# Linear attention plus MLP on one core: two more tiles turned without TensorE, and a normalisation moved to ScalarE

## The chip, the cores and the metric

The kernel runs on one core of one Trainium2 chip. The metric is device time in microseconds of one execution; a kernel's time is the median over several runs. A profiled execution has a time of its own, and inside it a span, from the first to the last recorded instruction.

## The reference

With `x` of 2048 tokens by 512 features, everything in float32:

```python
xn = layernorm(x)                                   # eps 1e-5, no scale, no shift
q, k, v = split(xn @ wqkv)                          # 32 heads of 16
phi = lambda t: where(t > 0, t + 1, exp(t)) + 1e-6
kv, z = sum_s phi(k)_s v_s^T, sum_s phi(k)_s        # per head
o = (phi(q) @ kv) / (phi(q) . z + 1e-6)
h = relu(xn @ w1 + b1) ** 2                         # 512 -> 1376
out = x + o @ wo + h @ w2 + b2
```

## The kernel before, in words

The tokens are 16 tiles of 128. Matrix products are done in three passes: each operand is split into a high half in the matmul's format and the rest (low half), and high x high, high x low and low x high are summed. So most operands have two instructions on the way to TensorE: a copy on ScalarE (`high`, the token tile's copy in `tokens`, the copy in `parts`) and a subtraction on VectorE or GpSimd.

The program first runs through the keys, tile by tile (lines 434 to 646), then through queries, attention and MLP. Only the key stage is touched. For one tile i it needs:

- statistics of the row (`measure`, L214 and L215, VectorE), the reciprocal root by Ln and Exp (`roots`, L225 and L226, ScalarE) with a Newton step on three narrow VectorE instructions (L234 to L236), and the normalisation itself, L242 on VectorE, into `xp[i]`;
- the turned tile (features on partitions): tiles 0 to 7 by four TensorE transposes into PSUM (`turned_pe`, L276), tiles 8 to 15 by `regroup` and `turn`: 16 moves between SBUF places for four tiles at once (`xg<-xp`, issued on SP at L258, 64 KB each), which put 32x32 blocks where they belong, and then one VectorE transpose of 32x32 blocks per tile (L262). `NPE` = 8 is that border;
- the turned tile's high half (`high`, L290, ScalarE) and low half (`low`, L293, VectorE), and for tiles 0 to 7 a copy to DRAM for later (`keep_t`, a ScalarE copy and an SP DMA at L299);
- `project` (L327): 12 matmuls into `pk`, the keys;
- `phi` on them: Relu (L318) and Exp (L320) on ScalarE, a sum on VectorE (L322), into `k`, and its halves in `parts` (L108 and L335);
- the token tile's halves in `tokens` (L108 ScalarE, L116 GpSimd), with the last column replaced by one and zero (L314, a small cast on GpSimd), which yields z;
- `kx` (L346): 12 matmuls that add phi(k)^T times the tokens into four banks. For tiles 0 to 7 they are ordered high x high, high x low, low x high, four each.

Each engine takes its instructions in the order in which the program issues them; a scheduler is switched off (`manual_schedule`). The loop at L610 writes that order out by hand: in round i TensorE projects tile i and does `kx` of tile i - 1; ScalarE does Relu, the high half of the next tile, Exp and the roots, and so on. `ahead` (L606) says of which tiles the statistics are taken at the end of a round, to be normalised in the next. `move(n)` (L255) puts up to n pending moves into SP's queue at the end of a round. `x4` and `x8` hold tiles 4 to 7 and 8 to 11 of the input; the load of `x4` is held back by a small GpSimd copy (L498). Buffers named `t` and `k` share six slots (tag `p`).

Of the kernel before, what the change touches and what calls it, by code (L numbers as in the profile page):

```python
# [18 lines left out]
def kernel(  # L19
# [29 lines left out]
    nc = tc.nc  # L49
    xf = x.rearrange("b s d -> (b s) d")  # L50
    of = out.rearrange("b s d -> (b s) d")
    S, D = xf.shape
    F = w1.shape[1]
    NT = S // P
    NJ = D // P
    TB = 4
    NB = NT // TB
    BT = TB * P
    NF = -(-F // P)
    NPE = 2 * TB  # L60
    WARM = 11
    NP = NF // 2
    FP = NF * P
# [5 lines left out]
    keep = ctx.enter_context(tc.tile_pool(name="keep", bufs=1))  # L69
    work = ctx.enter_context(tc.tile_pool(name="work", bufs=1))  # L70
# [35 lines left out]
    def copy(eng, o, i, bias=0.0):  # L106
        if eng == "act":
            nc.scalar.activation(o, i, AF.Copy, bias=bias)  # L108
        elif bias:
            ENG[eng].tensor_scalar(o, i, bias, None, op0=OP.add)  # L110
        else:
            ENG[eng].tensor_copy(o, i)

    def split(h, l, src, eh, el):
        copy(eh, h, src)
        ENG[el].tensor_tensor(out=l, in0=src, in1=f32(h), op=OP.subtract)  # L116
# [19 lines left out]
    xT = {b: keep.tile([P, NJ, BT], F32, name=f"xT{b}", tag=f"xT{b}") for b in range(NB // 2, NB)}  # L136
# [9 lines left out]
    heads = work.tile([P, P], F32, name="heads", tag="heads")  # L146
    b1s = keep.tile([P, NF], F32, name="b1s")
    zb = keep.tile([P, D], F32, name="zb")
    consts = keep.tile([P, 3, 1], F32R, name="consts")
    one_zero, eps = consts[:, :2], f32(consts[:, 2])  # L150

    xr, xp, xg, tok, pk, kp = {}, {}, {}, {}, {}, {}

# [53 lines left out]
    def group(*tiles):  # L207
        return tiles, *(small.tile([P, 3, k], F32, name=f"{n}{tiles[0]}", tag=n) for n, k in (("st", 6), ("mv", 2), ("y", 3)))
# [19 lines left out]
    def normalise(tiles, st, mv, y):  # L228

        n = len(tiles)  # L230
        var = mv[:, :n, 1]
        y0, u, r = (y[:, k, :n] for k in range(3))

        nc.vector.scalar_tensor_tensor(u, var, 1e-5, y0, op0=OP.add, op1=OP.mult)  # L234
        nc.vector.scalar_tensor_tensor(u, u, -0.5, y0, op0=OP.mult, op1=OP.mult)
        nc.vector.scalar_tensor_tensor(r, u, 1.5, y0, op0=OP.add, op1=OP.mult)  # L236
        for k, i in enumerate(tiles):
            o, src = xp[i], xr[i]
            if i >= NPE:

                o, src = o.rearrange("p g (j c) -> p g j c", j=NJ), gjc(src)
            nc.vector.tensor_scalar(o, src, mv[:, k, 0:1], r[:, k:k + 1], op0=OP.subtract, op1=OP.mult)  # L242
            if i in groups:
                regroup(*groups[i])

    def regroup(src, G):

        for r in range(NJ):
            for g in range(NJ):
                moves.append((G[32 * g:32 * (g + 1), r], src[32 * r:32 * (r + 1), g]))  # L250
        return G
# [8 lines left out]
    def turn(o, G):  # L260

        nc.vector.transpose(o.rearrange("p j (r t) -> p r j t", r=NJ),  # L262
                            G.rearrange("p r (j c) -> p r j c", j=NJ))

    def slot(i):
        return slice((i % TB) * P, (i % TB + 1) * P)

    def cols(i):

        return xsb[(i // TB + 1) % 2]  # L270

    def turned_pe(i):
        p = bank(f"pt{i}", "acc" if i < 3 else "ps")
        for j in range(NJ):
            at_j = slice(j * P, (j + 1) * P)
            nc.tensor.transpose(p[:, at_j], xp[i][:, at_j], ident)  # L276
        return p.rearrange("p (j t) -> p j t", j=NJ)

    def transposed(i, t=None):

        b, at = i // TB, slot(i)
        if i < NPE:
            t = t or turned_pe(i)
        else:
            t = xT[b][:, :, at]
            turn(t, xg[i])
        h, l = (x[:, :, at] for x in cols(i))

        def high():
            nc.scalar.activation(h, t, AF.Copy)  # L290

        def low():
            nc.vector.tensor_tensor(out=l, in0=t, in1=f32(h), op=OP.subtract)  # L293

        def keep_t():
            if i < NPE:
                k = w512(f"t{i}", "p", 6).rearrange("p (j t) -> p j t", j=NJ)
                copy("act", k, t)
                nc.sync.dma_start(xTd[b][:, :, at], k)  # L299

        return high, low, keep_t

    def run(*what):
        for f in what:
            f()

    def tokens(i):
        tok[i] = pair(f"tok{i}")
        h, l = tok[i][:, 0], tok[i][:, 1]
        src = xp[i]  # L310
        if i >= NPE:
            h, l, src = gjc(h), gjc(l), src.rearrange("p g (j c) -> p g j c", j=NJ)
        split(h, l, src, "act", "pool")
        nc.gpsimd.tensor_copy(tok[i][:, :, D - 1:], one_zero)  # L314

    def phi(ps, p, mid=lambda: None, late=lambda: None):

# [130 lines left out]
    nc.gpsimd.memset(f32(one_zero[:, 0]), 1.0)  # L448
    nc.gpsimd.memset(f32(one_zero[:, 1]), 0.0)
# [9 lines left out]
    pw = bank("warm")  # L459
    for _ in range(WARM):  # L460
        nc.tensor.matmul(pw[:, :P], lhsT=zb[:, :P], rhs=zb[:, :P], start=True, stop=True)

    groups = {}
    x4, x8 = four("x4", "r1"), four("x8", "r2")
    for i0 in range(0, NT, TB):
        a = first_xp[i0]
        if i0 < NPE:
            for k in range(TB):
                xp[i0 + k] = a[:, k]
        else:  # L470
            o = four(f"xg{i0}", "r0" if i0 + TB == NT else "r3")
            a, o = (t.rearrange("p a (g c) -> p (a g c)", g=NJ) for t in (a, o))
            groups[i0 + TB - 1] = [t.rearrange("p (g n) -> p g n", g=NJ) for t in (a, o)]
            a, o = (t.rearrange("p (g i c) -> p g i c", g=NJ, i=TB) for t in (a, o))
            for k in range(TB):
                xp[i0 + k], xg[i0 + k] = a[:, :, k], o[:, :, k]

    def heads_k(*js):
        for j in js:
# [63 lines left out]
    load_x(12, two("x12"))  # L543
    load_x(14, two("x14"))
    project(2, pks[2], wk, HL)
    soon = group(4, 8, 9)
    phi_k(0, pks[0])
    measure(soon, 0)
    tokens(0)
    parts(0)  # L550
    keep2()
# [51 lines left out]
                held.pop(0)()  # L603
            fetch()

    ahead = {3: (5, 10), 4: (6, 11), 5: (7, 12), 6: (13, 14), 7: (15,)}  # L606

    kxp = [bank(f"kx{c}", "acc") for c in range(NJ)]
    kx(0)
    for i in range(2, NT):  # L610
        if i == NPE:
            wq = both("wq", ("B0", "B1"))
        if i == 3:
            nc.sync.dma_start(b1s[:, :NF - 1], b1[:(NF - 1) * P].rearrange("(f p) -> p f", p=P))
# [6 lines left out]
        if i + 1 < NPE:  # L621
            high, low, keep_t = transposed(i + 1)
        k = NPE if i + 1 == NPE else i + 2
        turned = transposed(k) if i + 1 >= NPE and k < NT else ()

        def late():
            if soon:
                roots(*soon)
            low()

        phi_k(i, ps, high, late)
        run(*turned)
        if soon:
            normalise(*soon)
        parts(i)
        keep_t()
        if i == 2:
            tokens(2)
        if i + 1 < NT:
            tokens(i + 1)  # L640
        if i + 1 == NPE:
            run(*transposed(NPE + 1))
        pieces(2 if i >= NPE else 0)
        soon = statistics(*ahead[i + 1]) if i + 1 in ahead else ()
        move(8 if i >= NPE - 1 else 16)
        kx(i - 1)
# [98 lines left out]
    last = TB - 1  # L745
    w2r = [four(f"w2r{k}", f"C{k}", F32R, keep) for k in range(2)]
    for n in range(2):
        t1, t2 = NB - 1 - 2 * n, NB - 2 - 2 * n
        x1, x2 = xsb
        tag = "acc" if n else "ps"  # L750
# [207 lines left out]
        f = NF - 2  # L958
# [34 lines left out]
        for e, f in enumerate(waiting[:-2]):  # L993
# [22 lines left out]
            if e == NF - 4:  # L1016
                turned = attention_T(t2 * TB + 2)
# [53 lines left out]
```

## Time and profile before

| | |
|---|---|
| time, median of 3 runs | 424.54 us (423.74 to 424.91) |
| the profiled execution's own time | 423.9 us |
| its span | 422.2 us |
| TensorE matmul busy | 417.2 us, 99% of the span |
| VectorE, ScalarE, GpSimd busy | 71%, 59%, 8% |
| granted TensorE clock | 1.0 |
| DMA | 43.02 MB, 16 engines busy 34.4% on the main queue |

In the rows of a time line the columns are start, duration, engine, line, operation, result <- sources, the shapes and the count; in brackets stands the idle time of that engine just before, and what ended it. PE is TensorE's matmuls, PEld its weight loads, DVE VectorE, ACT ScalarE, POOL GpSimd, SPq the queue that issues DMAs. Several instructions of a kind in a row are merged into one row with their count. In a row of stretches, the first number is the length, then each engine's busy time and count of instructions, the granted clock, the busy share of the DMA engines and GB/s. The chain of work gives start, duration and what it was. In a row of groups the last part is busy time, mean ns of one, and idle time before with its releasers. A row of DMA issues ends with the microseconds from issue to landing.

### The profile page before, as it was taken

The page shows a single profiled execution, that of the slowest core. Times are in us where ns is not written, and L with a number is a line of the kernel's source. Part 1 is how long each engine was busy: PE and PEld are TensorE (multiplying, and loading weights), DVE is VectorE, ACT ScalarE, POOL GpSimd, SP SyncE. Part 2 cuts the span into 40 slices and gives each one's busy share as a digit, 9 for nine tenths or more (in the row PEclk, how much of TensorE's full clock was granted, in tenths as well). Part 3 has the DMA queues.
Part 4 walks back from the last instruction along what each step waited for, and adds up shares of the span by engine and source line. Part 5 has one row for each costly group of instructions (what it writes and reads, how often), then busy time and mean ns, then how long its engine had stood idle before and what let it go on. Part 6 is the DMA issues. An engine that isn't in the chain of part 4 may idle for free.

```text
span 422.2 us, 5377 instructions
## 1 busy us (share of the span) xinstructions
PE 417.2 (99%) x1868; PEld 344.8 (82%) x1868; DVE 299.0 (71%) x537; ACT 248.9 (59%) x441; POOL 33.2 (8%) x52
## 2 busy tenths in 40 slices
PE   8999999999999999999999999999999999999996
PEld 7788888888887888888888888888888888888885
DVE  6897788855668886777579376586977668577353
ACT  5766667645467777566466363666667665556140
POOL 3342333330000000000000000000000000000000
PEclk9999999999999999999999999999999999999999
DMA  7853437000412221536016652501120654023502
GB/s 248 282 157 82 105 105 230 16 0 2 112 50 63 88 73 52 184 84 182 0 57 196 190 201 76 144 0 50 51 75 25 200 99 152 1 88 96 160 0 99
DMA packets 42754, 43.02 MB, mean 102 GB/s; under 512 B 5828, under 2 KB 28612, under 8 KB 42472
## 3 DMA queue, kind: packets, MB, share of 16 engines
q1 hardware_dynamic: 42728, 42.69, 34.4%
q8 instruction: 14, 0.23, 0.2%
q14 instruction: 12, 0.10, 0.1%
HBM read 30.09 MB, written 6.29 MB: 86 GB/s over the span
## 4 chain that ended last, share of the span: by engine, by line
PE 97%; DVE 1%; DMA 1%; POOL 0%; ACT 0%; issue 0%; POOLq 0%
PE acc L127 38%; PE b L419 23%; PE kx L346 10%; PE pq L327 10%; PE pk L327 10%; PE pz L127 1%; PE b L127 1%; PE pkv L730 1%; PE pt L276 1%; PE pm L127 1%; DMA x<-in_A_x_dram 1%; PE end L127 0%; DVE st L214 0%; POOL tok L116 0%; DVE xp L242 0%; ACT k L320 0%
## 5 line engine op out<-in xcount | busy, mean ns | idle before, releaser
L127 PE MATMUL acc<-w2r,s 128*128 128x512 f32 x498 | 116.6, 389 | 0.0
L127 PEld LDWEIGHTS acc<-w2r,s 128*128 128x128 f32 x498 | 93.5, 188 | 19.6
L419 PE MATMUL b<-T,aop 128*128 128x512 f32 x240 | 59.6, 389 | 0.0
L419 PEld LDWEIGHTS b<-T,aop 128*128 128x128 f32 x240 | 45.0, 188 | 9.4
L346 PE MATMUL kx<-pk,tok 128*128 128x512 f32 x192 | 47.3, 394 | 0.1
L346 PEld LDWEIGHTS kx<-pk,tok 128*128 128x128 f32 x192 | 35.4, 188 | 8.3 <-POOL tok L314 1.1
L127 PE MATMUL acc<-mh,aTsr 128*128 128x512 f32 x96 | 30.3, 390 | 0.0
L108 ACT ACTIVATE w2r<-r 128x512 fp32r<-128x512 f32 x32 | 20.0, 625 | 13.5 <-PE acc L127 10.4
L119 DVE TENSOR_TENSOR w2r<-r,w2r 128x512 fp32r<-128x512 f32 x32 | 21.9, 686 | 7.3 <-ACT w2r L108 7.2
L419 PE MATMUL b<-xs0h,aop 128*128 128x512 f32 x80 | 26.4, 391 | 0.0
L116 POOL TENSOR_TENSOR tok<-xp,tok 128x512 fp32r<-128x512 f32 x16 | 22.1, 1379 | 53.6 <-ACT tok L108 53.6
L116 DVE TENSOR_TENSOR s<-c,s 128x512 fp32r<-128x512 f32 x20 | 13.9, 693 | 16.7 <-ACT s L108 16.7
L199 POOL MEMSET r<- 32x512 f32 x3 | 1.6, 522 | 278.1 <-DVE w2r L119 278.0
L322 DVE SCALAR_TENSOR_TENSOR q<-pq,q 128x512 f32<-128x512 f32 x16 | 11.0, 689 | 16.8 <-ACT q L320 16.8
L108 ACT ACTIVATE aop<-S 128x512 fp32r<-128x512 f32 x20 | 12.6, 629 | 14.7 <-DVE S L659 9.4
L127 PEld LDWEIGHTS acc<-mh,aTsr 128*128 128x128 f32 x96 | 18.0, 188 | 3.8
L860 DVE TENSOR_TENSOR res<-acc,res 128x512 f32<-128x512 f32 x16 | 11.0, 692 | 13.7 <-PE acc L127 13.7
L318 ACT ACTIVATE q<-pq 128x512 f32<-128x512 f32 x16 | 9.5, 591 | 18.4 <-PE pq L327 18.4
L318 ACT ACTIVATE k<-pk 128x512 f32<-128x512 f32 x16 | 9.5, 594 | 16.6 <-PE pk L327 16.5
L127 PE MATMUL acc<-ml,aTsr 128*128 128x512 f32 x48 | 18.7, 390 | 0.0
L419 PEld LDWEIGHTS b<-xs0h,aop 128*128 128x128 f32 x80 | 15.0, 188 | 3.4 <-ACT rz L407 0.3
L262 DVE STREAM_TRANSPOSE at<-g 128x512 f32<-128x512 f32 x16 | 10.5, 690 | 7.3 <-DMA g<-q 7.3
(190 smaller groups left out, 840.3 us busy)
## 6 DMA issues: line engine op xcount, KB each, us to landing
r<-in_B_w_dram SPq DMA_DIRECT2D x49, 256.0 KB, 3.2
res<-in_A_x_dram SPq DMA_DIRECT2D x8, 512.0 KB, 6.1
g<-q SPq DMA_DIRECT2D x64, 64.0 KB, 2.1
out_dram<-res SPq DMA_DIRECT2D x15, 256.0 KB, 2.1
x<-in_A_x_dram SPq DMA_DIRECT2D x5, 512.0 KB, 5.5
xTd<-t SPq DMA_DIRECT2D x8, 256.0 KB, 3.3
rq<-in_A_wqkv_dram SPq DMA_DIRECT2D x8, 256.0 KB, 5.9
xg<-xp SPq DMA_DIRECT2D x32, 64.0 KB, 2.0
```

The source lines that it names most:

```text
L108: nc.scalar.activation(o, i, AF.Copy, bias=bias)
L116: ENG[el].tensor_tensor(out=l, in0=src, in1=f32(h), op=OP.subtract)
L119: nc.vector.tensor_tensor(out=l, in0=src, in1=f32(h), op=OP.subtract)
L127: nc.tensor.matmul(ps, lhsT=a[u], rhs=b[v], start=first and n == 0, stop=last and n == 2)
L262: nc.vector.transpose(o.rearrange("p j (r t) -> p r j t", r=NJ), G.rearrange("p r (j c) -> p r j c", j=NJ))
L276: nc.tensor.transpose(p[:, at_j], xp[i][:, at_j], ident)
L318: nc.scalar.activation(p, ps, AF.Relu, scale=-1.0)
L322: nc.vector.scalar_tensor_tensor(p, ps, 0.0, p, op0=OP.max, op1=OP.add)
L327: nc.tensor.matmul(ps, lhsT=cols(i)[u][:, j, slot(i)], rhs=w[v][:, j, :], start=first and n == 0, stop=last and n == len(steps) - 1)
L346: nc.tensor.matmul(kxp[c], lhsT=tok[i][:, u, c * P:(c + 1) * P], rhs=pk[i][:, v], start=i == 0 and (u, v) == first, stop=i == NT - 1 and ( ...
L419: nc.tensor.matmul(ps, lhsT=a[u][:, j * P:(j + 1) * P], rhs=b[v][:, j, :], start=first and j == 0 and n == 0, stop=last and j == 1 and n == 2,
L860: nc.vector.tensor_tensor(out=r[:, a:z], in0=ps, in1=r[:, a:z], op=OP.add)
```

## The change

- Tiles 6 and 7 (`NDVE` = 6 up to `NPE` = 8) are normalised into a grouped layout, moved by 16 moves of 32 KB, and turned by VectorE into a buffer of tag `p`, which also goes to DRAM, so that the ScalarE copy for that is left out. Their eight TensorE transposes go.
- Tiles 8 to 15 are normalised on ScalarE: Identity with a scale and a bias per partition, the bias being -mean x reciprocal root, from one more narrow VectorE instruction per group. They are put at the end of the round's ScalarE work.
- The statistics come in other rounds: first 4, 6, 7 (was 4, 8, 9), then `ahead` as in the diff.
- Tile 8 is turned in round 6 (was round 7), 9 and the following in the round two before their own.
- The last column of a token tile is set to one by a GpSimd memset of `xp` before the halves are made, instead of a cast after them; the low half is then zero by itself. For tiles turned by TensorE it follows the transposes; for the others it comes with the tile before and waits for the moves that read it.

```diff
+    NDVE = NPE - 2
...
+        if tiles[-1] >= NPE:
+            nc.vector.scalar_tensor_tensor(u, mv[:, :n, 0], -1.0, r, op0=OP.mult, op1=OP.mult)
+        later = []
+
+        def last(i, o, src, k):
+            nc.scalar.activation(o, src, AF.Identity, bias=u[:, k:k + 1], scale=r[:, k:k + 1])
+            if i in groups:
+                regroup(*groups[i])
+
         for k, i in enumerate(tiles):
             o, src = xp[i], xr[i]
-            if i >= NPE:
+            if i >= NDVE:
                 o, src = o.rearrange("p g (j c) -> p g j c", j=NJ), gjc(src)
-            nc.vector.tensor_scalar(o, src, mv[:, k, 0:1], r[:, k:k + 1], op0=OP.subtract, op1=OP.mult)
-            if i in groups:
-                regroup(*groups[i])
+            if i < NPE:
+                nc.vector.tensor_scalar(o, src, mv[:, k, 0:1], r[:, k:k + 1], op0=OP.subtract, op1=OP.mult)
+                if i in groups:
+                    regroup(*groups[i])
+            else:
+                later.append(lambda a=(i, o, src, k): last(*a))
+        return later
...
         if i < NDVE:
             t = turned_pe(i)
         else:
-            t = xT[b][:, :, at]
+            t = xT[b][:, :, at] if i >= NPE else w512(f"t{i}", "p", 6).rearrange("p (j t) -> p j t", j=NJ)
             turn(t, xg[i])
...
+    def ones(i):
+        nc.gpsimd.memset(xp[i][:, D - 1:] if i < NDVE else xp[i][:, NJ - 1, P - 1:], 1.0)
...
         split(h, l, src, "act", "pool")
-        nc.gpsimd.tensor_copy(tok[i][:, :, D - 1:], one_zero)
+        if NDVE <= i + 1 < NT:
+            ones(i + 1)
...
-    soon = group(4, 8, 9)
+    soon = group(4, 6, 7)
...
-    ahead = {3: (5, 10), 4: (6, 11), 5: (7, 12), 6: (13, 14), 7: (15,)}
+    ahead = {3: (5, 8, 9), 4: (10, 11), 5: (12, 13), 6: (14, 15)}
...
-        k = NPE if i + 1 == NPE else i + 2
-        turned = transposed(k) if i + 1 >= NPE and k < NT else ()
+        turned = transposed(i + 2) if NDVE <= i + 1 and i + 2 < NT and i + 2 != NPE else ()
...
         run(*turned)
-        if soon:
-            normalise(*soon)
+        later = normalise(*soon) if soon else []
         parts(i)
         keep_t()
+        if i + 2 == NPE:
+            run(*transposed(NPE))
...
         if i + 1 < NT:
             tokens(i + 1)
-        if i + 1 == NPE:
-            run(*transposed(NPE + 1))
+        if i + 2 == NDVE:
+            run(*transposed(NDVE))
+        run(*later)
```

More of the change, by code (lines that the diff above doesn't have):

```diff
@@ L148 @@
     zb = keep.tile([P, D], F32, name="zb")
-    consts = keep.tile([P, 3, 1], F32R, name="consts")
-    one_zero, eps = consts[:, :2], f32(consts[:, 2])
+    eps = keep.tile([P, 1], F32, name="eps")
     xr, xp, xg, tok, pk, kp = {}, {}, {}, {}, {}, {}
@@ L276, in turned_pe, with transposed @@
             nc.tensor.transpose(p[:, at_j], xp[i][:, at_j], ident)
+        ones(i)
         return p.rearrange("p (j t) -> p j t", j=NJ)
-    def transposed(i, t=None):
+    def transposed(i):
         b, at = i // TB, slot(i)
-        if i < NPE:
-            t = t or turned_pe(i)
+        if i < NDVE:
+            t = turned_pe(i)
         else:
-            t = xT[b][:, :, at]
+            t = xT[b][:, :, at] if i >= NPE else w512(f"t{i}", "p", 6).rearrange("p (j t) -> p j t", j=NJ)
             turn(t, xg[i])
@@ L296, in keep_t @@
             if i < NPE:
-                k = w512(f"t{i}", "p", 6).rearrange("p (j t) -> p j t", j=NJ)
-                copy("act", k, t)
+                k = t
+                if i < NDVE:
+                    k = w512(f"t{i}", "p", 6).rearrange("p (j t) -> p j t", j=NJ)
+                    copy("act", k, t)
                 nc.sync.dma_start(xTd[b][:, :, at], k)
@@ L310, in tokens @@
         src = xp[i]
-        if i >= NPE:
+        if i >= NDVE:
             h, l, src = gjc(h), gjc(l), src.rearrange("p g (j c) -> p g j c", j=NJ)
         split(h, l, src, "act", "pool")
-        nc.gpsimd.tensor_copy(tok[i][:, :, D - 1:], one_zero)
+        if NDVE <= i + 1 < NT:
+            ones(i + 1)
     def phi(ps, p, mid=lambda: None, late=lambda: None):
@@ L447 @@
                             pattern=[[-1, P]], channel_multiplier=1)
-    nc.gpsimd.memset(f32(one_zero[:, 0]), 1.0)
-    nc.gpsimd.memset(f32(one_zero[:, 1]), 0.0)
     nc.gpsimd.memset(heads, 1.0)
@@ L466 @@
         a = first_xp[i0]
[L467 to L476, printed above, removed]
+        for k in range(TB):
+            xp[i0 + k] = a[:, k]
+        if i0 + TB <= NDVE:
+            continue
+        n = TB if i0 >= NPE else NPE - NDVE
+        o = work.tile([P, n, 512], F32, name=f"xg{i0}", tag="r0" if i0 + TB == NT else "r3" if i0 >= NPE else "ra")
+        a, o = (t.rearrange("p a (g c) -> p (a g c)", g=NJ) for t in (a[:, TB - n:], o))
+        groups[i0 + TB - 1] = [t.rearrange("p (g n) -> p g n", g=NJ) for t in (a, o)]
+        a, o = (t.rearrange("p (g i c) -> p g i c", g=NJ, i=n) for t in (a, o))
+        for k in range(n):
+            xp[i0 + TB - n + k], xg[i0 + TB - n + k] = a[:, :, k], o[:, :, k]
     def heads_k(*js):
@@ L620 @@
         high = low = keep_t = lambda: None
-        if i + 1 < NPE:
+        if i + 1 < NDVE:
             high, low, keep_t = transposed(i + 1)
-        k = NPE if i + 1 == NPE else i + 2
-        turned = transposed(k) if i + 1 >= NPE and k < NT else ()
+        turned = transposed(i + 2) if NDVE <= i + 1 and i + 2 < NT and i + 2 != NPE else ()
         def late():
```

## Prediction

> **What bounds the kernel now.** I read the page first, then the busy time by stretches, then the chain of work that ended last.
>
> ```profile
> span 422.2 us, 5377 instructions
> PE 417.2 (99%) x1868; PEld 344.8 (82%) x1868; DVE 299.0 (71%) x537; ACT 248.9 (59%) x441; POOL 33.2 (8%) x52
> ...
> 20.00:419.00 399.00, 398.95 (x1787) 329.89 (x1785) 283.51 (x499) 235.83 (x415) 27.18 (x35) 1.00 0.32 93
> ```
>
> From 20 to 419 us TensorE is busy 398.95 of 399.00 us at a granted clock of 1.00. So each microsecond taken off TensorE's own list there shortens the span by one, each new wait of TensorE lengthens it by one, and there is no later idle time that could absorb either. The place of the change is the key stage, where the chain alternates between twelve matmuls `pk` of one tile and twelve `kx` of the tile before, with four transposes `pt` between them as long as TensorE turns tiles:
>
> ```profile
> 35.40 2.72 PE pk L327 x12
> 38.12 0.44 PE pt L276 x4
> 38.56 2.75 PE kx L346 x12
> 41.31 2.72 PE pk L327 x12
> ...
> 47.25 2.72 PE pk L327 x12
> ...
> 52.69 2.72 PE pk L327 x12
> 55.41 2.72 PE kx L346 x12
> ```
>
> These `pk` are those of tiles 5, 6, 7 and 8, and the last `kx` is tile 7's. A period with transposes takes 5.91 us (35.40 to 41.31) and 5.94 (41.31 to 47.25), one without 5.44 (47.25 to 52.69).
>
> **Part 1, the transposes of tiles 6 and 7 go.** Both periods become 5.44: 0.47 + 0.50 = **0.97 us** less. Nothing hides this, since TensorE is the bound.
>
> **Part 2, ones by a memset.** Now a GpSimd cast behind the low half of each token tile holds up the first two `kx`:
>
> ```profile
> 15.98 0.63 ACT L108 ACTIVATE pk<-k 128x512 fp32r<-128x512 f32 x1 [0.24 <-DVE k L322]
> 16.67 0.53 PEld L346 LDWEIGHTS kx<-pk,tok 128*128 128x128 f32 x3 [0.18 <-ACT pk L108]
> 16.68 0.98 DVE L335 SCALAR_TENSOR_TENSOR pk<-k,pk 128x512 fp32r<-128x512 f32 x1
> 17.77 0.19 PEld L346 LDWEIGHTS kx<-pk,tok 128*128 128x128 f32 x1 [0.56 <-POOL tok L314]
> 19.43 0.63 ACT L108 ACTIVATE pk<-k 128x512 fp32r<-128x512 f32 x1 [0.23 <-DVE k L322]
> 20.27 0.53 PEld L346 LDWEIGHTS kx<-pk,tok 128*128 128x128 f32 x3
> 21.21 0.19 PEld L346 LDWEIGHTS kx<-pk,tok 128*128 128x128 f32 x1 [0.41 <-POOL tok L314]
> 23.16 0.19 PEld L327 LDWEIGHTS pk<-wkh,xs1h 128*128 128x128 f32 x1
> ```
>
> At 2.72 / 12 = 0.227 a matmul the fourth weight load would come at 17.35 and 20.95; it comes at 17.77 and 21.21, so 0.42 + 0.26 = 0.68 is lost. What is late next: tile 0's fifth matmul needs VectorE's low half, done at 17.66, and tile 1's `kx` needs ScalarE's high half, done at 20.06. So tile 1 starts near 20.13 whatever tile 0 gained, and twelve unhindered matmuls end at 22.85 instead of 23.16: **0.3 us** less, with bounds 0 and 0.68.
>
> The memset for tile 0 now stands on GpSimd ahead of the copy that releases the load of tiles 4 to 7, and waits for tile 0's transposes:
>
> ```profile
> 6.63 0.47 POOL L498 COPY x<-y 128x1 f32<-128x1 f32 x1 [4.03 <-DVE y L236]
> 7.03 0.60 ACT L290 ACTIVATE xs1h<-pt 128x512 fp32r<-128x512 f32 x1
> 15.87 0.68 DVE L214 BATCH_NORM_STATS2 st<-x 128x6 f32<-128x512 f32 x1
> ...
> x<-in_A_x_dram SPq DMA_DIRECT2D x1, 1024.0 KB, 6.6
> ```
>
> So that load leaves about 0.5 us later. With 6.6 us to landing it is there near 14.3, before the statistics at 15.87: nothing. Without that cover it would cost 0.5.
>
> **Part 3, what takes the transposes' place.** Tiles 6 and 7 are normalised where 8 and 9 were, then 16 moves of 32 KB go through SP's queue (ahead of the two bias loads and the stores of turned tiles 4 and 5, all wanted later), and VectorE turns the result. Moves and turns now:
>
> ```profile
> 23.61 1.46 DVE L242 TENSOR_SCALAR xp<-x,mv,y 128x512 f32<-128x512 f32 x3
> 34.55 0.15 DVE L234 SCALAR_TENSOR_TENSOR y<-mv,y 128x2 f32<-128x2 f32 x1
> ...
> 36.05 0.69 DVE L335 SCALAR_TENSOR_TENSOR pk<-k,pk 128x512 fp32r<-128x512 f32 x1
> 36.42 10.10 SPq L258 DMA_DIRECT2D xg<-xp  x16
> ...
> 61.15 4.95 SPq L258 DMA_DIRECT2D xg<-xp  x8
> 67.73 0.71 DVE L262 STREAM_TRANSPOSE xT<-xg 128x512 f32<-128x512 f32 x1 [0.26 <-issue]
> ...
> 180.48 11.77 SPq L258 DMA_DIRECT2D g<-q  x16
> ```
>
> SP issues one move per 0.63 us (10.10 / 16; 4.95 / 8 = 0.62). The last of the eight is issued at 61.15 + 7 x 0.62 = 65.5 and the turn that needs it starts at 67.73: 2.2 us from last issue to turn. Moves of 32 KB are not in this trace: I take 0.63 for them too (the nearest row, same engine, same 32 partitions), with bounds 0.57 (below that the end of VectorE's earlier work decides, see the rivals) and 0.73 (11.77 / 16). Tile 7's normalisation ends at 25.07, less the 0.3 of part 2; the first move goes at about 25.0, so the turn of tile 6 starts at 25.0 + 15 x 0.63 + 2.2 = **36.65**. Tile 6's own projection is wanted at 41.31 - 0.77 = 40.5 and has its high half by 38.1 (prices below): covered.
>
> What is queued behind that turn is the matter. ScalarE's list has, in order: high half of tile 6 (waits for the turn), then its new work, normalising tiles 10 and 11. Only then can the 16 moves of tiles 8 to 11 start, which now start at 36.42. Later, the high half of tile 8 waits for those moves, and behind it ScalarE has the token half of tile 7, the normalising of 14 and 15, and only then tile 7's own Relu and Exp, which TensorE's `kx` of tile 7 needs. Now ScalarE does these two first (50.01, 50.63), ahead of tile 8's half:
>
> ```profile
> 50.01 0.60 ACT L318 ACTIVATE k<-pk 128x512 f32<-128x512 f32 x1 [1.79 <-PE pk L327]
> 50.63 0.63 ACT L320 ACTIVATE k<-k 128x512 f32<-128x512 f32 x1
> 51.30 0.69 DVE L322 SCALAR_TENSOR_TENSOR k<-pk,k 128x512 f32<-128x512 f32 x1 [0.99 <-ACT k L320]
> 51.59 0.62 ACT L290 ACTIVATE xs1h<-xT 128x512 fp32r<-128x512 f32 x1
> 52.11 0.62 ACT L108 ACTIVATE pk<-k 128x512 fp32r<-128x512 f32 x1
> ...
> 55.43 0.70 DVE L262 STREAM_TRANSPOSE xT<-xg 128x512 f32<-128x512 f32 x1
> 56.16 0.63 ACT L290 ACTIVATE xs1h<-xT 128x512 fp32r<-128x512 f32 x1 [2.91 <-DVE xT L262]
> 290.31 0.72 ACT L407 ACTIVATE c<-c,b1s 128x512 f32<-128x512 f32 x1 [1.01 <-DVE c L884]
> 290.94 0.58 ACT L108 ACTIVATE t<-b 128x512 f32<-128x512 f32 x1
> ...
> L407 ACT ACTIVATE c<-c,b1s 128x512 f32<-128x512 f32 x10 | 7.3, 726 | 8.9 <-DVE c L884 8.9
> L108 ACT ACTIVATE tok<-xp 128x512 fp32r<-128x512 f32 x16 | 9.8, 618 | 0.0
> ```
>
> Prices: a turn's reader starts 0.73 after the turn (55.43 to 56.16); independent activations start 0.52 apart (51.59 to 52.11). A normalising activation, with bias and scale both per partition, is not in the trace. One with such a bias takes 0.726 against 0.618 without, 0.63 to the next start; with two I take 0.82 and 0.72 (bounds 0.62 and 0.90). The Trainium skill, "ScalarE: Activation LUTs", What ACT_TABLE_LOAD costs, gives 93 ns for each per-partition operand; the 108 ns above agree roughly, and its estimate of 0.80 would shorten the sum by under 0.1 us.
>
> The sum, from the turn of tile 6 at 36.65: high half +0.73, tile 10 +0.52, tile 11 +0.72, its end +0.82 (39.44); first move +0.1, last move +9.45, turn of tile 8 +2.2 = **51.2**. From there: its high half 51.93 to 52.55, `pk` of tile 8 by 52.68. TensorE wants it at 52.69 - 1.27 = 51.42: 1.26 lost. On ScalarE: tokens 52.45, tile 14 52.97, tile 15 53.69, tile 7's Relu 54.41, Exp 55.03 to 55.66, VectorE's sum 55.70 to 56.39, high half 56.44 to 57.06, `kx` of tile 7 at 57.2 (0.14 as from 15.98 + 0.63 to the first matmul after 16.67). Wanted at 55.41 - 1.27 = 54.14: **3.06 lost** in all, the first 1.26 included. In general the loss is the start of tile 8's turn less 48.14.
>
> Elsewhere: VectorE gives up eight normalisations and gets two turns and a narrow scale column per group. After tile 6's high half (38.0) its list to tile 5's low half has seven wide instructions of up to 0.69 (36.05) and six narrow ones of some 0.15 (34.55): 43.7, where the fifth matmul of tile 5's `kx` is wanted near 44.1, so no wait, with 0.4 to spare. The memsets for tiles 6 and 8 wait on GpSimd until the moves that read those columns have landed (36.5 and 51.1); the token halves behind them come at about 42 and 57. The moves of 12 to 15 now go without a break from 53.69 + 0.82 = 54.5 to 64.6, so a weight load that SP now issues just ahead of 61.15 goes some 4 us later, about when ScalarE, itself late, comes to it: nothing in the sum.
>
> Net: -0.97 - 0.30 + 3.06 = +1.8. The profiled execution took 423.9 around its span of 422.2; it becomes 425.7. The runs' median is 424.54, 0.64 above it, so I forecast **426.3** for the median: +0.42%. A difference of 0.3% (1.27 us) is about what a measurement here can tell from none.
>
> The Trainium skill, "VectorE: DVE Perf Modes", Rules for kernel authors, speaks against the change: it gives a 128x128 transpose to TensorE where PSUM may hold the result. By it the change loses, as in the sum; 0.44 us of `pt` stands against 16 issues of 0.63.
>
> **Rivals.** A, *the other side*: the queue is quick enough. If tile 8's turn can start by 48.1, ScalarE is never held, and the full 1.27 comes off: 423.27. That point needs a pitch of 0.49 per move for tiles 8 to 11 even with the earliest turn of tile 6 (48.1 - 35.7 - 2.9 - 2.2 = 7.3 over 15). For it: ScalarE is busy only 59% of the span. Against: 24 moves in a row at 0.62 to 0.63.
>
> B, smaller moves issue faster: at 0.57 or less the turn of tile 6 waits no longer for them but for VectorE's low half (it starts at 36.05 now, behind two normalisations of together 1.0 that go, and would end near 35.7). Tile 8's turn is then at 35.7 + 2.9 + 9.45 + 2.2 = 50.25, the loss 2.1, the time 425.4. Against: nothing shows that size matters for the pitch.
>
> C, moves at 0.73: tile 6's turn at 38.15, tile 8's at 52.7, the loss 4.56, the time 427.8.
>
> D, the change doesn't do what it says, the transposes being hidden already: the periods of 5.91 and 5.44 speak against it, and I give it nothing.
>
> **How the numbers follow.** Forecast 0.56, A 0.16, B 0.12, C 0.09, and 0.07 for what lies between A and B. Slower by over 0.3%: 0.54 of the forecast and C, 0.63. Faster: A with its startup gain between 0.3 and 0.68, 0.15. Within: B, the middle and the edges, 0.22. The range goes from A's 423.3 to C's 427.9, as the pitch of one move, times fifteen and twice in a row, carries it all.
>
> **What would show it.** Right: no `pt` of tiles 6 and 7; the first weight load of tile 3 near 22.85; 16 small moves over 10 us from 25; tile 8's turn near 51 after a wait for moves; ScalarE idle before that tile's high half, and TensorE waiting on ScalarE at `pk` of tile 8 and `kx` of tile 7, some 3 us together. Wrong: TensorE without idle between 40 and 60 us (A), a shorter pitch of the small moves (B), or waits in another place.

## The result and the profile after

| | before | after |
|---|---|---|
| time, median | 424.31 us (423.74 to 424.91, 4 runs) | 427.47 us (426.94 to 427.86, 4 runs) |
| the profiled execution's own time, its span | 423.9, 422.2 us | 427.3, 425.6 us |

The ratio of the runs is 1.0078, 95% interval 1.0066 to 1.0089; the medians lie 3.2 us apart (1.0074). So it is slower. The forecast was 426.3, 1.8 above the median then known (424.54). The page of the changed kernel begins with the span and the busy time:

```profile
span 425.6 us, 5376 instructions
PE 417.1 (98%) x1860; PEld 344.2 (81%) x1860; DVE 296.9 (70%) x532; ACT 253.0 (59%) x445; POOL 27.5 (6%) x50
```

TensorE's work did not grow; it even lost eight transposes. So the time went into waits. Two stretches of the changed kernel say where (columns: length, then busy time and count of TensorE, weight loads, VectorE, ScalarE and GpSimd, the granted clock, DMA):

```profile
20.00:62.00 42.00, 38.85 (x174) 30.92 (x173) 32.11 (x73) 30.50 (x60) 11.10 (x16) 1.00 0.46 120
62.00:419.00 357.00, 357.00 (x1589) 295.52 (x1588) 247.90 (x418) 209.72 (x360) 11.22 (x18) 1.00 0.31 90
```

All of it lies between 20 and 62 us: 3.15 us without a matmul, and none after 62. The same stretch of the kernel before has no such time:

```profile
20.00:62.00 42.00, 42.00 (x195) 34.46 (x194) 35.43 (x79) 27.57 (x59) 14.67 (x18) 1.00 0.41 110
```

TensorE's time line of the changed kernel in that stretch names the waits. Its rows of `pk` are the first matmuls of tiles 6, 7, 8 and 9:

```profile
40.67 0.39 PE L348 MATMUL pk<-wkh,xs0h 128*128 128x512 f32 x1
...
45.10 2.11 PE L367 MATMUL kx<-pk,tok 128*128 128x512 f32 x8 [0.64 <-DVE pk L356]
47.05 0.40 PE L348 MATMUL pk<-wkh,xs0h 128*128 128x512 f32 x1
...
53.72 0.50 PE L348 MATMUL pk<-wkh,xs1h 128*128 128x512 f32 x1 [1.06 <-ACT xs1h L304]
...
58.19 3.06 PE L367 MATMUL kx<-pk,tok 128*128 128x512 f32 x12 [1.45 <-ACT pk L109]
61.08 0.39 PE L348 MATMUL pk<-wkh,xs1h 128*128 128x512 f32 x1
```

The same work in the kernel before, `pk` of tile 8, `kx` of tile 7 and `pk` of tile 9:

```profile
52.53 0.39 PE L327 MATMUL pk<-wkh,xs1h 128*128 128x512 f32 x1
...
55.25 2.88 PE L346 MATMUL kx<-pk,tok 128*128 128x512 f32 x12
57.97 0.39 PE L327 MATMUL pk<-wkh,xs1h 128*128 128x512 f32 x1
```

A period without transposes takes 5.44 there (52.53 to 57.97), and half of one 2.72. Set beside that, the waits cost 0.94 (tile 5's `kx`, after its first four matmuls: 47.05 less 40.67 is 6.38), 1.23 (tile 8's `pk`), 1.75 (tile 7's `kx`) and 0.17 in its course, together 4.09. Less the 0.97 of the transposes, tile 9's `pk` starts 3.11 later (61.08 against 57.97). The idle times in brackets add up to 3.15 only: each matmul's row lasts 0.39, while the next one starts 0.23 after it, so beside a wait some of the loss counts as busy (4.09 less 3.15 here). That is why the busy time of the page fell by 0.1 only, though 0.97 of transposes are gone. The last matmul ends 3.06 later (422.02 against 418.96) and the span 3.4.

The chain of work that ended last runs through exactly what was put in the transposes' place (start, duration, what):

```profile
34.92 1.88 DMA xg<-xp
...
36.98 0.72 DVE t L275
37.72 0.63 ACT xs0h L304
38.35 1.42 ACT xp L242 x2
...
46.76 1.49 SPq L271
...
50.20 1.97 DMA xg<-xp
...
52.29 0.72 DVE xT L275
...
54.19 1.41 ACT xp L242 x2
```

Read downwards: the last of the small moves lands, tile 6 is turned and its high half made, only then does ScalarE normalise tiles 10 and 11, only then do the moves of tiles 8 to 11 begin, and the last one lands just before tile 8's turn at 52.29. Then comes another pair of normalisations on ScalarE (tiles 14 and 15), ahead of tile 7's Relu. The rows of SP's queue give the pitch:

```profile
25.36 10.14 SPq L271 DMA_DIRECT2D xg<-xp  x16
...
39.79 10.99 SPq L271 DMA_DIRECT2D xg<-xp  x16
```

The first sixteen carry 32 KB each, the second 64 KB: 0.63 us apiece for both, apart from one of the second group that took 1.49. The page lists a DMA queue `q8 instruction`, with 14 packets over the span. One of these is under way when that issue begins (the packet starts at 46.61 and takes 1.27, the issue starts at 46.76).

The first of the three waits is of another kind. The time line of all engines around it:

```profile
43.13 1.30 POOL L117 TENSOR_TENSOR tok<-xp,tok 128x512 fp32r<-128x512 f32 x1 [5.16 <-DVE y L236]
...
43.17 1.27 DVE L238 SCALAR_TENSOR_TENSOR y<-mv,y 128x2 f32<-128x2 f32 x1
...
44.37 0.68 DVE L356 SCALAR_TENSOR_TENSOR pk<-k,pk 128x512 fp32r<-128x512 f32 x1
44.48 1.52 ACT L242 ACTIVATE xp<-x,y 128x512 f32<-128x512 f32 x2 [1.43 <-DVE y L238]
```

A VectorE instruction on 128x2 numbers, 0.16 us elsewhere, takes 1.27 and ends at 44.44, within 0.01 of GpSimd's subtraction (43.13 + 1.30). Tile 5's low half is queued behind it, and ScalarE's normalising waits for it. The Trainium skill, "SBUF — State Buffer", SBUF: two separate sides, says that a VectorE instruction with two inputs in SBUF and a GpSimd one that reads SBUF exclude each other, and that whichever starts first keeps the port to its end. By that rule this trace agrees: 1.27 against 0.16.

### The profile page after: what moved, and what is told of

Same layout as the page of the kernel before. It is cut to its first block, busy times and chain, and to the rows that moved or that the text cites. A ratio compares the mean times of both kernels' runs of the same rounds, so it can differ in the third digit from the quotient of the medians.

```text
span 425.6 us, 5376 instructions
## 1 busy us (share of the span) xinstructions
PE 417.1 (98%) x1860; PEld 344.2 (81%) x1860; DVE 296.9 (70%) x532; ACT 253.0 (59%) x445; POOL 27.5 (6%) x50
## 4 chain that ended last, share of the span: by engine, by line
PE 88%; SPq 4%; DVE 3%; ACT 2%; DMA 1%; issue 1%; DVEq 0%
PE acc L128 38%; PE b L440 22%; PE pq L348 10%; PE pk L348 6%; PE kx L367 6%; SPq L271 4%; PE pz L128 1%; PE b L128 1%; PE warm L480 1%; DMA xg<-xp 1%; PE pkv L752 1%; ACT xp L242 1%; PE pm L128 1%; DVE pk L356 1%; DVE k L343 0%
## 5 line engine op out<-in xcount | busy, mean ns | idle before, releaser
L343 DVE SCALAR_TENSOR_TENSOR k<-pk,k 128x512 f32<-128x512 f32 x16 | 11.0, 685 | 8.9 <-ACT k L341 8.9
```

Source lines behind the costliest of these rows:

```text
L343: nc.vector.scalar_tensor_tensor(p, ps, 0.0, p, op0=OP.max, op1=OP.add)
```

## The experiments

Theory: the loss is the lateness of tile 8's turn. That is 16 issues of 0.63 us on one queue, begun behind ScalarE's normalising, and then ScalarE's in-order list, where tile 8's half and two normalisations stand ahead of tile 7's Relu. Rivals: that the waits add up one by one, that normalising on ScalarE costs by itself, or that the transposes' time was never there to gain. Each ratio below is against runs of the kernel before on the same chip. Lines of kernels with one more constant are shifted by one.

**1. Tile 7's Relu first** (tile 8 turned in round 7, as before):

```diff
-        turned = transposed(i + 2) if NDVE <= i + 1 and i + 2 < NT and i + 2 != NPE else ()
+        k = NPE if i + 1 == NPE else i + 2
+        turned = transposed(k) if NDVE <= i + 1 and k < NT and i + 2 != NPE else ()
...
-        if i + 2 == NPE:
-            run(*transposed(NPE))
...
+        if i + 1 == NPE:
+            run(*transposed(NPE + 1))
```

> From the changed kernel, only the order: tile 8 is turned in round 7 again, so that ScalarE has tile 7's Relu and Exp ahead of tile 8's high half. My theory (the loss is set by the start of tile 8's turn, 52.29 us in the changed kernel's profile, and by what stands behind its high half on ScalarE): the wait of pk of tile 8 stays (1.2 us), that of kx of tile 7 (1.75 us) goes, so about 425.7 us against 427.5. Rival (ScalarE's added load as such costs the time, 8 activations of 0.8): the work is the same, so no change, 427.5.

Measured: 425.56 us, ratio 1.0038 (1.0023 to 1.0053), where the changed kernel has 1.0078. ScalarE's time line of this run:

```profile
50.11 0.57 ACT L339 ACTIVATE k<-pk 128x512 f32<-128x512 f32 x1
50.71 0.63 ACT L341 ACTIVATE k<-k 128x512 f32<-128x512 f32 x1
53.15 0.63 ACT L304 ACTIVATE xs1h<-xT 128x512 fp32r<-128x512 f32 x1 [1.80 <-DVE xT L275]
```

Tile 8's turn still starts at 52.40. But Relu and Exp now stand ahead of the half that waits for it, and tile 7's `kx` waits for nothing. So the 1.75 at that `kx` came from ScalarE's order alone.

**2. Tile 5's parts first** (removes the wait of tile 5's `kx`):

```diff
+        if i == NDVE - 1:
+            parts(i)
         later = normalise(*soon) if soon else []
-        parts(i)
+        if i != NDVE - 1:
+            parts(i)
```

> From the changed kernel, only the order: in round 5 the halves of tile 5's keys stand ahead of the narrow scale instructions on VectorE. The wait of TensorE at kx of tile 5 (1.07 us in the profile) should go in any case. My theory: the time stays at 427.5 within 0.3, since tile 8's turn starts no sooner (52.3) and pk of tile 8 then waits about 2.2 instead of 1.2 us. Rival (each wait of TensorE counts by itself): 426.5.

Measured: 427.35 us, ratio 1.0077 (1.0062 to 1.0092). TensorE's waits in this run (total, times, longest):

```profile
PE pk L348 <- ACT xs1h L304: 1.6, 1, 1.6
PE kx L367 <- ACT pk L109: 1.5, 1, 1.5
```

Tile 5's wait is gone and the time is unchanged. Counted by starts as above, tile 8's `pk` now loses 2.24 instead of 1.23 (it starts 7.68 after tile 7's, 46.39 to 54.07), and tile 7's `kx` 1.75 as before: the waits are not additive. What sets the end is the later of the two, tile 8's turn.

**3. The queue cleared** (ScalarE normalises 10 and 11 ahead of tile 6's half; the store of tile 6 and the bias loads go behind the moves of 8 to 11):

```diff
-        if i + 2 == NDVE:
-            run(*transposed(NDVE))
         run(*later)
+        store_6 = lambda: None
+        if i + 2 == NDVE:
+            h6, l6, store_6 = transposed(NDVE)
+            run(h6, l6)
...
         move(8 if i >= NPE - 1 else 16)
+        store_6()
...
-        if i == 3:
+        if i == NPE:
             nc.sync.dma_start(b1s
```

> From the changed kernel, only the order: on ScalarE the normalising of tiles 10 and 11 stands ahead of tile 6's high half, and on SP the store of turned tile 6 and the two bias loads stand behind the moves of tiles 8 to 11. My theory: these moves start at about 38.0 instead of 39.8 us, tile 8's turn at 50.5 instead of 52.3, so 1.8 us less, 425.7. Rival (ScalarE's added load): the same work, no change, 427.5.

Measured: 425.96 us, ratio 1.004 (1.0026 to 1.0054). Here the moves start at 38.23 and the turn at 51.01:

```profile
38.23 10.08 SPq L271 DMA_DIRECT2D xg<-xp  x16
```

That is 1.28 sooner than in the changed kernel, and this execution began 0.24 later than that of before. The prediction's formula (start of tile 8's turn less 48.14) reckons with a start that is 0.30 sooner, by part 2; this one is 0.24 later. Without the one and with the other it gives 51.01 - 48.14 - 0.30 - 0.24 = 2.33. Tile 7's `kx` starts at 56.90 instead of 55.25, and 56.90 - 55.25 - 0.24 + 0.97 = 2.38. By tile 9's `pk` (59.76 instead of 57.97) the loss is 2.52. The waits are at other places than in the changed kernel: 1.17 at tile 5's `kx`, none at tile 8's `pk`, and 0.77 at tile 7's `kx`.

**4. All normalising back on VectorE**, tiles 6 and 7 still moved:

```diff
+    NACT = 16
...
-        if tiles[-1] >= NPE:
+        if tiles[-1] >= NACT:
...
-            if i < NPE:
+            if i < NACT:
```

> From the changed kernel, tiles 8 to 15 are normalised on VectorE again; tiles 6 and 7 are still turned by moves. My theory: the moves of tiles 8 to 11 still queue on SP behind the store of turned tile 6 (about 38.9), tile 8's turn starts near 50.8, and behind its high half ScalarE has only the tokens: kx of tile 7 at about 55.4 instead of 58.2, so some 2.8 us less, 424.7, not better than before. Rival (ScalarE's load was the whole loss): the transposes' gain shows, 423.3.

Measured: 424.92 us, ratio 1.0021 (1.0011 to 1.003). The moves of 8 to 11 start at 38.56. The wait that TensorE shows is tile 5's `kx`, here because of a normalisation itself. GpSimd's and VectorE's time lines:

```profile
42.78 1.29 POOL L118 TENSOR_TENSOR tok<-xp,tok 128x512 fp32r<-128x512 f32 x1 [4.97 <-ACT tok L110]
...
42.83 2.00 DVE L253 TENSOR_SCALAR xp<-x,mv,y 128x512 f32<-128x512 f32 x2
44.75 0.68 DVE L357 SCALAR_TENSOR_TENSOR pk<-k,pk 128x512 fp32r<-128x512 f32 x1
...
51.05 0.71 DVE L276 STREAM_TRANSPOSE xT<-xg 128x512 f32<-128x512 f32 x1 [1.21 <-DMA xg<-xp]
```

Two normalisations that together take 1.00 at 48.24 take 2.00 here, and tile 5's low half, next in line, makes TensorE wait 1.39. It is not the only thing that is late: tile 8's turn still waits for the moves. In the changed kernel tile 8's `pk` starts 1.43 after that turn (52.29 to 53.72), which would give about 52.5 here (an estimate); it starts at 52.90, behind the late `kx`. So most of this loss would have come at tile 8's `pk` if it had not come before. No wait of TensorE for ScalarE is left, and the time is close to the 424.7 of the theory.

**5. Two queues**: the changed kernel, every second move of 8 to 11 issued by GpSimd.

```diff
-                nc.sync.dma_start(*moves.pop(0))
+                (nc.gpsimd if two and len(moves) % 2 else nc.sync).dma_start(*moves.pop(0))
...
-        move(8 if i >= NPE - 1 else 16)
+        move(8 if i >= NPE - 1 else 16, i == 4)
```

> As the changed kernel, but every second one of the 16 moves of tiles 8 to 11 is issued by GpSimd's queue instead of SyncE's. Theory (16 moves at one every 0.63 us on one queue set the turn of tile 8): the last move goes out about 5 us sooner, tile 8's turn no longer waits (at or under 48), the waits of tile 8's pk and of tile 7's kx are gone and only the wait in tile 5's kx (0.94 us) stays: 424.2 us. No issue on GpSimd's queue shows in any trace so far: if one took over 1.1 us there, the turn would come at 50 and the time would be 425.9 or more. Rival (normalising on ScalarE itself holds TensorE up, whatever the queue): 426.5 to 427.5.

Measured: 425.41 us, ratio 1.0031 (1.002 to 1.0042); 424.2 was expected. The queue's part came true, the rest did not. SP's, GpSimd's and VectorE's time lines:

```profile
39.70 5.32 SPq L271 DMA_DIRECT2D xg<-xp  x8
...
39.98 4.07 POOL L271 DMA_DIRECT2D xg<-xp  x8 [2.06 <-ACT xp L242]
...
43.20 2.71 DVE L356 SCALAR_TENSOR_TENSOR pk<-k,pk 128x512 fp32r<-128x512 f32 x1
...
49.64 0.71 DVE L275 STREAM_TRANSPOSE xT<-xg 128x512 f32<-128x512 f32 x1
```

The last move goes out near 45 instead of 50, the turn waits for no move (no bracket), and the waits of tile 8's `pk` and tile 7's `kx` are gone. But GpSimd's subtraction now comes right behind its issues (44.07 to 45.36) and meets tile 5's low half itself: that begins while GpSimd still issues and ends 0.55 after the subtraction, 2.71 instead of 0.69. By the starts on record this is not the order of the Trainium skill's rule above: the low half began 0.87 before the subtraction. Nor do the issues alone explain it: in run 12 a low half at 41.32, amid GpSimd's issues, took 0.69. What held it at first stays open. Tile 7's `pk` starts 1.86 late and stays so. The Trainium skill, "DMA: Bandwidth & Descriptors", Rules for kernel authors, says that spreading transfers over issuing engines gains no bandwidth and only saves issue time. Here issue time was what was short: 5.32 for SP's eight against 10.99 for sixteen.

**6. The ones alone** (4's edit and the one below, with the rounds and `ahead` of before, so that only the memset is left of the change):

```diff
-    NDVE = NPE - 2
+    NDVE = NPE
+    NACT = NT
```

> The kernel before with the memset of the ones alone; all else as before. Theory: the stretch from the first matmul of tile 0's pk to that of tile 3's is 15.4 us instead of 15.7, as in all five traces with the memset, and that comes out at the end: 0.3 under the kernel before, about 423.7. Rival (the gain of the start is an accident of when tile 0's data arrived, or is given back later): the stretch stays at 15.7, or the time stays at 424.0.

Measured: 423.84 us, ratio 0.9995 (0.9987 to 1.0004): not distinguishable from no change. In the trace the stretch from tile 0's first `pk` matmul to tile 3's is 15.46, against 15.70 (7.68 to 23.38) before:

```profile
8.17 1.02 PE L349 MATMUL pk<-wkh,xs1h 128*128 128x512 f32 x2
...
23.63 0.39 PE L349 MATMUL pk<-wkh,xs1h 128*128 128x512 f32 x1
```

All thirteen traces with the memset have 15.37 to 15.46, so 0.24 to 0.33 are gained there. But where the stretch begins varies from 7.64 to 8.28 among executions of the same start, and that covers it.

**7. VectorE for 8 to 11, and the queue cleared** (the edits of 2 and 3, and 4's with another border):

```diff
+    NACT = 12
```

> Tiles 6 and 7 turned by moves, tiles 8 to 11 normalised on VectorE and 12 to 15 on ScalarE; the store of tile 6 and the bias loads behind the moves of 8 to 11 on SyncE's queue; in round 5 tile 5's pk low half ahead of the normalising. Theory: the moves of 8 to 11 start at 36.2, right behind those of 6 and 7, tile 8's turn comes at 48.3 (0.2 to 0.5 after it would be free of waits), tile 5's kx waits for nothing: 0.97 and 0.3 gained, 0.3 to 0.5 lost to the turn and 0.3 at the last store: 423.4 to 423.7. Rival (the removed transposes were hidden anyway, or VectorE is now too full in rounds 4 and 5): 424.0 to 425.

**8. The same with two queues** (5's edit on top):

```diff
-        move(8 if i >= NPE - 1 else 16)
+        move(8 if i >= NPE - 1 else 16, i == 4)
```

> As the run with tiles 8 to 11 on VectorE and the cleared queue, and every second move of tiles 8 to 11 issued by GpSimd's queue too. Theory: tile 8's turn comes at about 43.5, well ahead of its time; no wait on TensorE from tile 3 on; 0.97 and 0.3 gained, 0.3 lost at the last store at most: 423.0 to 423.2. Rival (the issue on GpSimd's queue delays its subtractions, so that tile 6's kx waits): 424 or more, with a wait of TensorE for GpSimd.

Measured: 424.92 (1.0021, 1.0012 to 1.003) and 425.36 (1.003, 1.0018 to 1.0041); both theories missed. The times fall where the rivals had them, but TensorE waits for ScalarE, which neither rival named, and by the same mechanism in both. In 8 the last move begins to be issued at 41.57, and yet tile 8's turn comes at 49.94. ScalarE's time line in 8:

```profile
45.00 1.52 ACT L243 ACTIVATE xp<-x,y 128x512 f32<-128x512 f32 x2 [2.06 <-DVE y L239]
46.43 0.58 ACT L340 ACTIVATE k<-pk 128x512 f32<-128x512 f32 x1
...
51.75 1.51 ACT L243 ACTIVATE xp<-x,y 128x512 f32<-128x512 f32 x2
53.16 0.57 ACT L340 ACTIVATE k<-pk 128x512 f32<-128x512 f32 x1
```

Tiles 12 and 13 are normalised at 45.00, after a wait for VectorE's narrow instructions (the first of them takes 1.25, beside GpSimd's subtraction again). Tile 6's Relu stands behind them, VectorE's sum and low half of tile 6 behind that (to 49.84), and then the turn. One round on it is the same for tile 7's Relu (53.16), and TensorE waits for ScalarE 0.23 at tile 6's `kx` and 0.99 at tile 7's. So the rival has its share: with the queue out of the way, normalising on ScalarE costs by its place ahead of Relu.

**9. ScalarE's normalising alone** (as 6, with tiles 8 to 15 on ScalarE):

```diff
-    NACT = NT
+    NACT = NPE
```

> The kernel before, with the memset of the ones and with tiles 8 to 15 normalised on ScalarE; tiles 6 and 7 stay with TensorE's transposes and the rounds of the statistics stay as before. Theory (normalising on ScalarE costs TensorE time only where it stands ahead of a Relu that TensorE's next product needs and ScalarE has no idle time left): in the kernel before ScalarE idles 1.8 us ahead of each Relu of rounds 4 and 5, the two normalisations take 1.4, so no new wait shows: 423.7 to 424.0. Rival (it always costs, as the last run suggests): a wait of TensorE for ScalarE's pk of 0.5 to 1.0 in one or two rounds, 424.5 to 425.5.

Measured: 424.47 us, ratio 1.001 (1.0001 to 1.0019), between the two expectations and 0.6 above run 6. No wait in rounds 3 to 9. The one wait is 0.43 at tile 10's `kx`, and it comes through the moves again: those of 12 to 15 start at 57.27 (before: 54.98), and VectorE waits for them at tile 12's turn:

```profile
70.03 0.71 DVE L276 STREAM_TRANSPOSE xT<-xg 128x512 f32<-128x512 f32 x1 [2.28 <-DMA xg<-xp]
```

**10 and 11. All on VectorE, tiles 12 to 15 one round later** (with 3's and 4's edits), on one queue and, with 5's edit, on two:

```diff
-    ahead = {3: (5, 8, 9), 4: (10, 11), 5: (12, 13), 6: (14, 15)}
+    ahead = {3: (5, 8, 9), 4: (10, 11), 6: (12, 13), 7: (14, 15)}
...
+        if i >= NDVE - 1:
+            parts(i)
         later = normalise(*soon) if soon else []
-        parts(i)
+        if i < NDVE - 1:
+            parts(i)
```

> All tiles normalised on VectorE, tiles 6 and 7 turned by moves, SyncE's queue cleared, a round's pk low half ahead of its normalising from round 5 on, and tiles 12 to 15 measured and normalised one round later, so that round 5 has none. Theory (the remaining losses of the last runs are engine time in rounds 5 and 6: ScalarE's 1.4 us ahead of Relu, VectorE's queue in round 5): no wait of tiles 5 to 7's kx; tile 8's turn at 48.5 to 49.5, as the moves still go out one every 0.63 us; 0.3 to 1.0 lost there: 423.6 to 424.2. Rival (the moves of tiles 6 and 7 cost whatever the order, through the queue or the buffers): 424.9 as before.

> As the run with tiles 12 to 15 one round later, and every second move of tiles 8 to 11 issued by GpSimd's queue. Theory: nothing is late any more, every period of rounds 5 to 8 is 5.44 us; 0.97 and 0.3 gained, 0.33 lost at the end: 423.0 to 423.2, faster than both kernels. Rival (a wait that the other runs have covered): 423.8 or more, with a wait of TensorE between 43 and 62 us that is in none of the other runs.

Measured: 429.83 (1.0127, 1.0112 to 1.0141) and 428.63 (1.0105, 1.0091 to 1.0119). Both missed, and 11 shows why. The first matmuls of tiles 3 and 11 there:

```profile
23.44 0.39 PE L349 MATMUL pk<-wkh,xs1h 128*128 128x512 f32 x1
...
67.93 0.39 PE L349 MATMUL pk<-wkh,xs1h 128*128 128x512 f32 x1
```

Between them TensorE waits for nothing: 44.49 us for eight periods, where the kernel before takes 45.47 (23.38 to 68.85). **That difference of 0.98 is the transposes' 0.97 in full.** Then tile 12's turn is late. VectorE's and TensorE's time lines in 11:

```profile
71.84 0.71 DVE L276 STREAM_TRANSPOSE xT<-xg 128x512 f32<-128x512 f32 x1 [3.22 <-DMA xg<-xp]
...
73.93 4.36 PE L368 MATMUL kx<-pk,tok 128*128 128x512 f32 x12 [3.12 <-ACT pk L110]
```

Tiles 14 and 15 one round later made the moves of 12 to 15 go out in two halves, from 57.5 and 64.8. Run 10 has the same wait, and before it one at tile 8's turn for moves that one queue issues. In run 11 that wait costs more than its length: the twelve matmuls behind it take 4.36 (2.88 is usual), and the granted clock from 73.9 to 78.4 is 0.65. In run 10's profiled execution it is 1.00 from 75.6 to 78.7, behind a wait of 3.50, and that execution, 428.40, is the quickest of its four.

**12. The same, with those moves out in one round** and on two queues, the bias loads in round 12:

```diff
-        move(8 if i >= NPE - 1 else 16, i == 4)
+        move(8 if i >= NPE else 16, i in (4, 7))
```

> As the run with tiles 12 to 15 one round later and two queues, but their 16 moves go out in one round, every second one from GpSimd's queue too, and the bias loads on SyncE's queue in round 12. Theory: in that run TensorE waited for nothing from tile 3's pk to the end of tile 11's, 0.98 us ahead of the kernel before, and lost it all at the turn of tile 12, whose moves were 5 us late; with these gone out by 65 us the turn comes at 67.5 to 68 instead of 71.8, nothing waits, and the time is 423.0 to 423.3: 0.97 from the transposes, 0.3 from the ones, less 0.33 at the end. Rival (the matter goes on round by round: what is pulled out of one round makes the next late): a wait of TensorE after 68 us that is in no other run, 424 or more.

Measured: **423.0 us**, ratio 0.9974 (0.9963 to 0.9984): faster than the kernel before, and so than the changed one. Normalising is all on VectorE here and tiles 12 to 15 come a round later, so of the change as made the turned tiles 6 and 7 and the ones are left. A stretch of this run, then SP's, GpSimd's and VectorE's time lines in two further fences:

```profile
20.00:62.00 42.00, 42.00 (x191) 34.53 (x191) 36.65 (x80) 27.23 (x55) 19.95 (x31) 1.00 0.44 121
```

```profile
57.75 5.57 SPq L272 DMA_DIRECT2D xg<-xp  x8
...
57.98 4.01 POOL L272 DMA_DIRECT2D xg<-xp  x8 [1.71 <-DVE xp L253]
```

```profile
48.75 0.70 DVE L276 STREAM_TRANSPOSE xT<-xg 128x512 f32<-128x512 f32 x1
...
67.95 0.71 DVE L276 STREAM_TRANSPOSE xT<-xg 128x512 f32<-128x512 f32 x1
```

TensorE is busy 42.00 of 42.00 again. Neither tile 8's turn nor tile 12's has a wait in front of it. From tile 3's `pk` the last matmul ends 394.58 later (23.69 to 418.27), against 395.58 (23.38 to 418.96) before.

## Why the prediction was right, and where its sizes were off

The forecast was slower, 426.3 in a range of 423.3 to 427.9; it came out slower, at 427.47. Step by step:

- **Part 1** held: 0.97. The period of tile 5 to 6 is 5.44 in the changed kernel, and runs 11 and 12 bring the whole amount out. Rival D was rightly given nothing.
- **Part 2** held in its stretch: 0.25 in the trace after (15.45 for 15.70), 0.24 to 0.33 in all, for the 0.3 taken. The sum over one execution did not show it, because tile 0's first `pk` matmul started 0.25 later there. Run 6 does not resolve it in the median.
- **Part 3** held in mechanism and place: moves, tile 6's turn, two normalisations, moves, tile 8's turn, then tile 8's `pk` and tile 7's `kx`. Two normalising activations take 1.51 (0.72 + 0.82 = 1.54 was taken), and the small moves go out 0.63 apart (as taken, so rivals B and C are out). The formula (turn less 48.14) reckons with the 0.30 of part 2, which this execution did not have; without it, it gives 3.85 for the turn at 52.29. Up to the start of tile 7's `kx` the waits are 3.92, and 0.17 more come in its course.
- The term that was mis-sized is that turn, 51.2 in the prediction. Tile 6's turn was 0.33 later, of which 0.30 is the sooner start that did not come; from there to the first move 0.08 less; the sixteen moves took 0.96 more, 0.9 of it in the single issue of 1.49; the landing 0.11 less. So the loss was 4.09 instead of 3.06. The prediction took every issue at 0.63, though the trace before has such a long issue too, a store of 1.08 at 46.62.
- "With 0.4 to spare" for tile 5's low half failed: its first use waited, 0.94 lost. The prediction counted VectorE's instructions but not that GpSimd's subtraction holds one of them. The hold stands in a row that it quoted: a low half of 0.98 at 16.68, where others take 0.69, and GpSimd's subtraction was under way. The miss does not enter the sum (run 2). In run 5 a low half that is held is the only wait left; in run 4 it falls together with the late turn.
- The end grew by another 0.3, from the last matmul's end to the span's end (the span grew by 3.4, the last matmul's end by 3.06). Nothing in the sum stood for that, and its cause was not tried.

The shortfall of the net, 3.4 in the profiled execution for the 1.8 predicted, is thus 1.03 of waits, 0.3 of start and 0.3 of end. The way and the place were right. The number is inside the range but nearer to rival C's 427.8 than to the forecast, and C's ground, a pitch of 0.73 for the small moves, is not in the trace.

Rival A, "the full 1.27 comes off: 423.27", named what would be needed, a turn of tile 8 in time. Run 12 meets it by two queues instead of a quicker one, with normalising back on VectorE and the rounds of tiles 12 to 15 shifted, and gets 423.0, 1.03 below its own runs of before. The Trainium skill, "VectorE: DVE Perf Modes", Rules for kernel authors, gives a 128x128 transpose to TensorE where PSUM may hold the result. The runs show both sides of that: the change as made, which goes against the rule, loses 3.2 us, and run 12, which goes against it too, gains 1.0.

## What to carry to other kernels

Work taken off the bounding engine is gained only if each deadline that it had is met by what replaces it. Write down, for the replacement, the queue's issues times their pitch and everything that stands ahead in each in-order list, up to the moment when the bound engine needs the result. New work on a half-idle engine belongs behind the instruction that the bound engine waits for next; 59% busy says nothing about that. And one repaired wait uncovers the next: here five (the queue, ScalarE's order, VectorE behind GpSimd, ScalarE's order again, the next group's moves) lay between a loss of 3.2 us and a gain of 1.0.

## What the runs showed of the hardware that was not expected

- Some VectorE instructions that overlap GpSimd's 128x512 subtraction are done only behind it. A 128x2 one took 1.27 for 0.16 and ended with it. Low halves end 0.55 later: 0.98 for 0.69 at 16.68 in the kernel before (the subtraction ended at 17.11), 2.71 in run 5. In run 4 two normalisations took 2.00 for 1.00 together. Others are not held: in the changed kernel the statistics of a tile at 31.98 took 0.66 beside the subtraction of 31.27 to 32.56, and a low half that began ahead of one (58.22 against 58.74) took 0.69.
- GpSimd issues a move of 64 KB every 0.51 us (4.07 for eight), SP every 0.63, whether of 32 or 64 KB.
- In several kernels one of the sixteen moves of tiles 8 to 11 takes 1.3 to 1.9 us on SP (1.49 after, 1.87 in run 1, 1.62 in run 2, 1.29 in run 4), and in others none (10.08 for sixteen in run 3). In each trace one `q8 instruction` packet starts between 45.6 and 48.3 us, and the SP issue that begins while it is under way, or up to 0.1 ahead of it, is the long one, where there is such an issue; in the kernel before and in run 3 that is a store (1.08 and 1.11). That the packet is the cause was not tried.
- Behind a wait of 3.12 us TensorE's granted clock fell to 0.65 in run 11, and behind one of 3.50 it stayed at 1.00 in the profiled execution of run 10. What decides it was not tried.
- The same start code brings tile 0's first product anywhere between 7.64 and 8.28 us, which is more than the ones gain.
